# DeltaNet attention into a gated feed-forward: w_out converted in front of the second substitution, and chunk 1's first slots without feed-forward

## The chip, the cores and the metric

The kernel runs on one core of a Trainium2 chip. The metric is the device time of one execution in microseconds (us). The profile is of one further execution, taken by the hardware profiler. The engines are TensorE (PE: matmuls and, as PEld, their weight loads), VectorE (DVE), ScalarE (ACT), GpSimd (POOL) and SyncE (SP), whose instructions here are all DMAs. [...]

## The reference

There are 4 batches (b), 8 heads (h), 768 steps and a head size of 48. The attention keeps a 48x48 state for each of the 32 batch-head pairs and updates it at every step; its output, laid out as 3072 tokens of 384, goes through a feed-forward with a quick GELU. The weights arrive as 64-bit floats.

```python
k_n = k / (norm(k) + 1e-06)
for t in range(S):
    y[t] = q[t] @ state
    v_old = k_n[t] @ state
    state = state + beta[t] * outer(k_n[t], v[t] - v_old)
x = y.transpose(0, 2, 1, 3).reshape(B * S, H * D)
h = x @ w_in                       # 3072x384 @ 384x2048
out = (h / (1 + exp(-1.702 * h))) @ w_out   # 2048x384
```

## The kernel before

The 768 steps are cut into 6 chunks of 128. A *unit* is one chunk of one batch (8 heads together); units 0 to 3 are chunk 0, units 4 to 7 chunk 1, and so on up to 23. The recurrence within a chunk is a triangular system. Its matrix has four diagonal blocks of 32; these are inverted on DVE, and the rest is done by forward substitution on PE.

**Keys.** For each unit the keys are normalised in place (`normalize`, lines 301 to 315, mostly on POOL, or `normalize_mixed`, 317 to 330, on ACT and DVE), turned on PE (`turn`: tile psT, then kT), and multiplied with themselves (`gram`: psG, then G). `prepare` (402 to 434) does the last two, and sends G's diagonal blocks through DRAM (Nd) into the tile NT, one partition for each block and row group. Key tiles KN rotate through 7 buffers; a key tile is loaded by `load` (84 to 90).

**Inversion, called the second substitution for chunk 1.** `invert` (441 to 537) is a chain of DVE operations on NT and YB: multiply NT by beta, 15 rounds for the 16-wide diagonal halves, 4 + 4 rounds (`dots`) for the quarter between them, then the result YS. For chunk 0 the result is turned on DVE (YT) and scaled into XB; later chunks send YS through DRAM (Yd) into XB, the factor that the first matmul of a hop (psU) needs. `invert(0)` and `invert(1)` treat four units at once, later calls two.

**Hops.** `together` (796 to 810) is one hop: psU = XB times V for a block (`solve`, copied by ACT into U), and psR = G times U for the blocks below (`below`), which DVE subtracts from V (`rest`). Each hop needs the copy and the subtraction of the one before.

**Slots.** `woven(n, share)` (840 to 881), called slot n below, runs three hops, each serving up to three units at different blocks, and between them the work for later units: psQ of unit n+1 (line 858), `prepare` of unit n+5, rounds of `invert` (STEPS, line 837) when n is 5 or more, the outputs of unit n-1 (psY), and psT of the queries of unit n+2. `follow(n)` (812 to 827) issues loads and, for even n from 6, queues the feed-forward of a finished pair of units.

**Feed-forward.** `hidden` (700 to 722) computes the 2048 hidden values of a pair of units in 16 items of three matmuls (ph, then gT by ACT's GELU); `written` (724 to 739) and `both_written` (741 to 759) compute the outputs in 16 items of two or four matmuls (po, copied by ACT to o, stored by SP). `spend(cost)` (831 to 835) lets the queued items into a slot up to a cost of 1.3 for each item.

**Conversion.** The weights' 64-bit words are turned into float32 by `conversion` (205 to 228): one AND on DVE, one Relu on ACT, and four more DVE operations for each piece. w_in has 9 pieces, w_out 14 (`pieces`, 230 to 251); `fill` (294 to 296) emits the next operations in order. Raw slices of w_out land in places that earlier pieces leave, so most are fetched when an earlier one is done (`fetches`, 283 to 291): slice 3 after the last of w_in, 8 to 15 after slices of w_out.

**Order of the work around the change.** Nearly all of it is pinned to the order in which the code emits it. First come norms and keys of chunk 0, `invert(0)` with a block of filler matmuls (`warm`, which multiply constants and whose result nobody reads; NY = 60 of them at line 501), 8 hops for units 0 and 1, 8 hops for units 2 and 3 with hidden of the first pair between them, and `keys` (962 to 982), which works through the keys of units 4 to 8 by a table of begins. Then (lines 1033 to 1051) the rest of w_in is converted, `invert(1)` is emitted between items of hidden, and slots 3, 4, 5 ... follow, of which slots 3 to 6 carry the po items of chunk 0's two pairs, and `both_written` draws the conversion of w_out along with it. `feed` emits one item of feed-forward.

```python
    while not ("in", 3, 1) in done:
        fill(2)
        feed()
        ahead_of(preparing, 1)
```

Of the kernel before, what the change touches and what calls it, by code (L numbers as in the profile page):

```python
# [18 lines left out]
def kernel(  # L19
# [26 lines left out]
    NP = H // 2  # L46
# [8 lines left out]
    GB = 8  # L55

    XR = DP - D
    NW, NA, NY, NU = 14, 3, 60, 11
    NQ = DFF // 4
    NPC = DFF // 8  # L60
    NS = C * C + C
# [379 lines left out]
    def invert(c, b0=0, nb=B):  # L441

        np = nb * NB * H
        part = slice(b0 * NB * H, b0 * NB * H + np)
        N, Y = NT[part], YB[part]
        bc = bI[part, c].broadcast_to([np, BS, BS])
        tt, red = vec.tensor_tensor, vec.tensor_reduce
        if c > 0:
            tt(N, N, bc, op=ALU.mult)
            yield 0.0  # L450
        HS = BS // 2

        def dots(o, a, b, ny, nx, nk, negate):

            P = wk.tile([128, ny, nx, nk], F32, tag="P", name="P")[part]
            tt(P, a, b, op=ALU.mult)
            red(o, P, axis=AX.X, op=ALU.add, negate=negate)

        def halves(t):

            return [t[:, s * HS : (s + 1) * HS, s * HS : (s + 1) * HS] for s in range(2)]


        Yf = Y.rearrange("p j i -> p (j i)")
        Nf = N.rearrange("p i k -> p (i k)")
        step = HS * BS + HS

        def diag(t, off, dims):
            return bass.AP(t.tensor, t.offset + off, [t.ap[0], [step, 2]] + dims)

        for i in range(1, HS):
            P = wk.tile([128, 2, i, i], F32, tag="P", name="P")[part]
            tt(
                P, diag(Nf, i * BS, [[0, i], [1, i]]), diag(Yf, 0, [[BS, i], [1, i]]),
                op=ALU.mult,
            )
            red(diag(Yf, i, [[BS, i]]), P, axis=AX.X, op=ALU.add, negate=True)
            yield 0.0


        X1 = N[:, 0:HS, HS:]
        if c == 1:
            vec.tensor_copy(X1, halves(Y)[1].rearrange("p l i -> p i l"))
        else:
            act.activation(X1, halves(Y)[1].rearrange("p l i -> p i l"), ACT.Copy)
        A = N[:, 0:HS, 0:HS]
        N10, Y0 = N[:, HS:, 0:HS], halves(Y)[0]
        Q = 4
        for j in range(0, HS, Q):
            n = HS - j  # L490
            dots(
                A[:, j : j + Q, :],
                N10[:, :, j:].rearrange("p (o l) k -> p o l k", o=1).broadcast_to([np, Q, HS, n]),
                Y0[:, j : j + Q, j:].rearrange("p j (o k) -> p j o k", o=1).broadcast_to([np, Q, HS, n]),
                Q, HS, n, False,
            )
            yield 0.0
        for i in range(0, HS, Q):
            n = i + Q
            if c == 0 and i == HS - 2 * Q:  # L500
                warm(NY, vec.memset)
            dots(
                Y[:, 0:HS, HS + i : HS + i + Q],
                A[:, :, 0:n].rearrange("p j (o l) -> p j o l", o=1).broadcast_to([np, HS, Q, n]),
                X1[:, i : i + Q, 0:n].rearrange("p (o i) l -> p o i l", o=1).broadcast_to([np, HS, Q, n]),
                HS, Q, n, True,
            )
            yield 0.0
        if c == 0:
            T = wk.tile([128, BS, BS], F32, tag="P", name="YT")  # L510
            vec.transpose(T.rearrange("p d i -> p i d"), Y.rearrange("p j i -> p i j"))
            for b in range(B):
                XB = wk.tile([128, H, BS], F32, tag="XB", name="XB", bufs=4)
                tt(
                    XB, T[:, b * H : (b + 1) * H],
                    zs[:, 5, b].broadcast_to([128, H, BS]), op=ALU.mult,
                )
                inverse[b] = XB
                yield 0.0
            return  # L520
        YS = wk.tile([128, BS, BS], F32, tag="P", name="YS")[part]
        tt(YS, Y, bc, op=ALU.mult)
        dma = sync if c < 3 else nc.sync.dma_start
        groups = [range(b0, b0 + nb)]
        back = {}
        for bs in groups:
            for b in bs:
                back[b] = dram.tile([H * C, BS], F32, tag="Yd", name="Yd", bufs=4)
                dma(
                    out=back[b].rearrange("(p j) i -> p j i", j=BS),  # L530
                    in_=YS[(b - b0) * NB * H : (b - b0 + 1) * NB * H],
                )
            for b in bs:
                XB = wk.tile([128, H, BS], F32, tag="XB", name="XB", bufs=4)
                dma(out=XB, in_=back[b].rearrange("(h t) i -> t h i", h=H))
                inverse[c * B + b] = XB
        yield 0.0
# [162 lines left out]
    def hidden(xT, gT, t, cost, gated=False):  # L700

        n = t.stop - t.start
        for f0 in range(0, FC, 2):
            if f0 // FQ == len(gT):
                gT.append(wk.tile([128, FQ, NTH], F32, tag="gT", name="gT", bufs=GB))
            if gated:
                while not ready_in(f0):
                    fill(1)
            ph = ps_moe.tile([128, 2, n], F32, tag="moe", name="ph")
            for u in range(2):  # L710
                f = f0 + u
                for j in range(KC):
                    pe.matmul(
                        ph[:, u], lhsT=w_in[:, j, f * 128 : (f + 1) * 128], rhs=xT[:, j, t],
                        start=(j == 0), stop=(j == KC - 1),
                    )
                if u == 0:
                    yield cost
            act.activation(
                gT[f0 // FQ][:, f0 % FQ : f0 % FQ + 2, t], ph, ACT.Gelu_apprx_sigmoid  # L720
            )
            yield cost
# [48 lines left out]
    def run(work):  # L771
        for _ in work:
            pass
# [38 lines left out]
    def follow(n):  # L812

        dma = sync if n <= B else nc.sync.dma_start
        if n + B < len(units):
            load(n + B, ((QP, q),), dma)
        m = n - 1 + len(KN)
        if m < len(units):
            load(m, ((KN, k),), nc.gpsimd.dma_start)
        if n - 1 + B < len(units):  # L820
            load_values(n - 1 + B, dma)
        if n % HB == 0 and n > B:
            h = (n - 1) // HB
            gT = []
            queue.append(hidden(xTs[h], gT, slice(0, NTH), 1.3))
            queue.append(written(*units[h * HB], gT))
            xTs.pop(h)

    debt = [0.0]

    def spend(cost):

        debt[0] = debt[0] + cost if queue else 0.0
        for done in take(debt[0]):
            debt[0] -= done
# [71 lines left out]
    for b in range(B):  # L907
        load_values(b, sync)
    fetch_in(1, other_queue)
    D_ = spare("blocks").rearrange("p (b h k) -> p b h k", b=B, k=BS)  # L910
    fetch_in(2, other_queue)
    for n in range(B, len(KN)):
        load(n, ((KN, k),), sync)
# [13 lines left out]
    norms_first()  # L927
    for e in range(2):
        vec.tensor_tensor(
            D_[:, :, e::2], psD[e], zs[:, 5, :, e::2].broadcast_to([128, B, NP, BS]), op=ALU.mult  # L930
        )
    vec.transpose(
        NT.rearrange("p i k -> p k i"), D_.rearrange("p b h k -> p k (b h)")
    )
    for b in range(B):
        gram(b)
# [25 lines left out]
    def keys():  # L962

        def unit(n):
            yield from normalize_mixed(n)
            yield from prepare(n)

        begun[2 * B] = prepare(2 * B)

        def first(n):  # L970
            yield from normalize_mixed(n)
            next(begun[n])

        work = [unit(n) for n in range(B, 2 * B)] + [first(2 * B)]
        for t in range(26):
            for u, begin in enumerate((0, 3, 6, 14, 17)):
                s = t - begin
                if s >= 0 and s % 2 == 0:
                    next(work[u], None)
            yield  # L980
        for w in work:
            run(w)
# [43 lines left out]
    for s in pair[2:]:  # L1026
        put_out(s)
        feed()
        fill(2)
    ffn.append(hidden(xTs[1], gTs[1], slice(0, NTH), 1.3, True))  # L1030
    xTs.pop(0), xTs.pop(1)
    load(B + 2, ((QP, q),), sync)
    while not ("in", 3, 1) in done:
        fill(2)
        feed()
        ahead_of(preparing, 1)
    run(preparing)
    first = new_step(B)
    run(first.scored)
    inverting = invert(1)  # L1040
    for i in range(25):
        ahead_of(inverting, 1)
        feed()
    run(inverting)
    fill(5)
    while ffn:
        feed()
    queue = [both_written(0, gTs[0]), written(*units[HB], gTs[1])]
    for n in range(B - 1, len(units) + 1):
        woven(n, 20.8 if n > 6 else 10.4)  # L1050
    run(take(1e9))
# [31 lines left out]
```

## Time and profile before

| what | value |
|---|---|
| median of 3 runs | 792.73 us (790.88 to 793.82) |
| profiled execution: its own time | 792.6 us |
| profiled execution: span, first to last instruction | 790.9 us |
| mean granted TensorE clock | 0.965 of full |
| PE busy, 0 to 51 us (norms, first inversion) | 39.7 of 51.05 us, clock 0.67 |
| PE busy, 51 to 103 us (hops of chunk 0) | 49.5 of 51.75 us |
| PE busy, 103 to 121 us (hidden, rest of w_in) | 17.6 of 18.6 us |
| DVE busy, 103 to 121 us | 13.0 of 18.6 us |
| filler matmuls | 199 |

The table of stages gives, for each stretch, the time that each engine was busy and in brackets its instructions, then the clock that was granted to TensorE, the share of the DMA engines and the rate of transfer. A line of the timeline gives start, duration, engine, source line, operation, tiles written and read, their shapes and the count, and in square brackets how long the engine had been idle before it and what released it. Line 102 is a helper through which most instructions pass, so groups are told apart by tile. The trace counts a float32 matmul as two records.

### The profile page before, as it was taken

What the parts mean: (1) busy time and instruction counts of PE and PEld (TensorE: products, weight loads), DVE (VectorE), ACT (ScalarE), POOL (GpSimd) and SP (SyncE); (2) the same over time, 40 slices, a digit from 0 to 9 for tenths busy, and PEclk for the clock granted to TensorE, in tenths of its full rate; (3) what the DMA queues carried; (4) which work ended last, traced back from release to release, by engine and by line L of the source; (5) the groups of instructions that cost most, each with busy time, mean ns of one, the idle gap of its engine ahead of it and who ended that gap; (6) DMA issues with size and microseconds to landing.
All of it is one profiled execution on the core that took longest, in us unless ns stands there. A gap on an engine that the chain in (4) does not pass through costs nothing.

```text
span 790.9 us, 18899 instructions
## 1 busy us (share of the span) xinstructions
PE 754.1 (95%) x8199; PEld 564.5 (71%) x8199; DVE 456.5 (58%) x934; ACT 243.0 (31%) x537; POOL 127.1 (16%) x132
## 2 busy tenths in 40 slices
PE   7788999598899999999999999999999999999997
PEld 6677888355568768768678678678678678677684
DVE  6778778996895666766666766756756531100000
ACT  4555552244233323223223223223223123121110
POOL 6301410001121212212212211221210000000000
PEclk8589999799999999999999999999999999999999
DMA  9941940453323231231222232241230020000000
GB/s 164 176 58 39 256 96 8 111 162 72 75 64 70 55 86 42 58 90 35 64 74 52 56 95 43 46 103 42 46 76 12 21 43 2 12 15 1 25 1 20
DMA packets 130657, 50.72 MB, mean 64 GB/s; under 512 B 105408, under 2 KB 126016, under 8 KB 130576
## 3 DMA queue, kind: packets, MB, share of 16 engines
q1 hardware_dynamic: 128112, 41.08, 24.1%
q0 software_dynamic: 2464, 8.46, 4.4%
q8 instruction: 64, 1.05, 0.6%
q14 instruction: 17, 0.14, 0.1%
HBM read 32.08 MB, written 16.25 MB: 61 GB/s over the span
## 4 chain that ended last, share of the span: by engine, by line
PE 81%; DVE 12%; DMA 3%; ACT 2%; issue 2%; SPq 1%; POOL 0%; DVEq 0%; POOLq 0%; ACTq 0%
PE po L102 28%; PE ph L102 26%; PE psY L102 5%; PE psU L102 5%; PE psQ L102 4%; PE psG L102 4%; PE ps_warm L102 3%; PE psT L102 3%; DVE P L102 3%; DVE YB L102 2%; DVE w_out L102 2%; PE psR L102 2%; DVE tmp L102 2%; DMA Nd<-G 1%; DVE NT L102 1%
## 5 line engine op out<-in xcount | busy, mean ns | idle before, releaser
L102 PE MATMUL po<-w_out,gT 128*128 128x384 f32 x768 | 269.5, 500 | 11.7 <-ACT w_out L102 8.9
L102 PE MATMUL ph<-xT,w_in 128*128 128x256 f32 x1152 | 261.5, 383 | 0.3
L102 PEld LDWEIGHTS ph<-xT,w_in 128*128 128x128 f32 x1152 | 214.7, 190 | 32.7 <-issue 1.5
L102 PEld LDWEIGHTS po<-w_out,gT 128*128 128x128 f32 x768 | 143.1, 193 | 103.9 <-ACT w_out L102 9.3
L102 DVE TENSOR_TENSOR V<-V,psR 64x384 f32<-64x384 f32 (+1 forms) x96 | 53.4, 556 | 198.0 <-PE psR L102 192.7
L102 ACT ACTIVATE gT<-ph 128x512 f32<-128x512 f32 x96 | 56.5, 596 | 140.1 <-PE ph L102 140.0
L102 DVE TENSOR_TENSOR P<-NT,YB 64x8 f32<-64x8 f32 (+31 forms) x190 | 89.2, 469 | 5.3
L102 ACT COPY US<-psU 32x384 f32<-32x384 f32 x92 | 43.2, 469 | 146.1 <-PE psR L102 128.6
L102 DVE TENSOR_REDUCE YB<-P 64x4 f32<-64x8 f32 (+31 forms) x190 | 80.9, 426 | 6.5
L102 PEld LDWEIGHTS psU<-V,XB 32*32 32x32 f32 x1536 | 57.9, 106 | 35.4 <-issue 29.0
L102 PE MATMUL psU<-V,XB 32*32 32x48 f32 x1536 | 68.6, 204 | 1.5 <-DVE YB L102 1.2
L605 POOL TENSOR_SCALAR_AFFINE_SELECT M<-M 128x1024 f32<-128x1024 f32 x20 | 24.9, 1247 | 265.9 <-DVE M L102 169.4
L102 PE MATMUL psR<-US,G 32*32 32x48 f32 x2208 | 60.4, 204 | 0.0
L102 PEld LDWEIGHTS psR<-US,G 32*32 32x32 f32 x2208 | 51.1, 106 | 1.1 <-ACT G L102 0.5
L102 PE MATMUL psQ<-QS,kT 48*128 48x176 f32 (+1 forms) x384 | 37.6, 341 | 3.7 <-ACT QS L102 3.7
L102 DVE TENSOR_TENSOR P<-NT 64x256 f32<-64x256 f32 (+7 forms) x40 | 34.0, 851 | 4.8 <-ACT NT L102 4.6
L102 PEld LDWEIGHTS psQ<-QS,kT 48*128 48x128 f32 x384 | 31.1, 209 | 6.8 <-ACT QS L102 5.6
L102 PE MATMUL ps_warm<-ident 128*128 128x256 bf16 x199 | 29.9, 309 | 5.4 <-DVE ps_warm L102 4.0
L102 PE MATMUL psG<-kT 48*128 48x128 f32 x384 | 32.3, 306 | 2.6 <-ACT kT L102 1.3
L102 DVE TENSOR_REDUCE NT<-P 64x64 f32<-64x1024 f32 (+7 forms) x40 | 32.6, 815 | 1.4
L87 POOL DMA_DIRECT2D KN<-in_k_dram x15 | 14.3, 951 | 111.5 <-PE psY L102 102.6
L102 PEld LDWEIGHTS psG<-kT 48*128 48x128 f32 x384 | 27.3, 205 | 6.0 <-ACT G L102 2.1
(98 smaller groups left out, 604.2 us busy)
## 6 DMA issues: line engine op xcount, KB each, us to landing
Nd<-G SPq DMA_DIRECT2D x16, 512.0 KB, 3.5
QP<-in_q_dram SPq DMA_DIRECT2D x24, 192.0 KB, 3.8
V<-in_v_dram SPq DMA_DIRECT2D x24, 192.0 KB, 3.3
out_dram<-o SPq DMA_DIRECT2D x24, 192.0 KB, 1.9
KN<-in_k_dram POOLq DMA_DIRECT2D x15, 192.0 KB, 3.7
NT<-Nd SPq DMA_DIRECT2D x20, 128.0 KB, 2.5
Yd<-YS SPq DMA_DIRECT2D x20, 128.0 KB, 2.4
XB<-Yd SPq DMA_DIRECT2D x20, 128.0 KB, 3.3
```

The costliest lines, as they stand in the source:

```text
L87: dma(out=dst[n % len(dst)][:, :, 0:D], in_=src[b, :, c * C : (c + 1) * C, :].rearrange("h p d -> p h d"),)
L102: return lambda *a, **kw: tc.keep_in_program_order(op(*a, **kw))
L605: (pool if self.n < B else nc.gpsimd).affine_select(out=self.M, in_=self.M, compare_op=ALU.is_gt, fill=0.0, base=0, pattern=[[0, H], [1, 1 ...
```

## The change

Six things change.

1. **Fillers at the start.** 48 filler matmuls in place of 60, released one round of the loop earlier (the third of the last four rounds from the end instead of the second).
2. **Layouts of two DVE transposes.** The tile YT is now written densely and read with a stride by the four operations after it; the tile "blocks" is written with a stride by the two operations before its transpose and read densely by it.
3. **Keys of units 7 and 8** begin 4 steps earlier in `keys`, and it has 22 steps instead of 26.
4. **Keys of units 9 and 10** are loaded by SP ahead of the slots, instead of by POOL in `follow`, and normalised ahead of `invert(1)` by `more_keys`; unit 9's are also turned there. Slots 4 and 5 then find `prepare` begun.
5. **All of w_out is converted ahead of `invert(1)`**, with both hiddens and both po passes of chunk 0 between the operations; scores of unit 4 (psT, psQ) come at the start of that loop.
6. **Slots 3 to 6 have no feed-forward.** `spend` emits fillers (3.8 for each unit of cost, 37 in a slot) until `follow(6)` queues the first pair of chunk 1.

```diff
-    NW, NA, NY, NU = 14, 3, 60, 11
+    NW, NA, NY, NU = 14, 3, 48, 11
...
-            if c == 0 and i == HS - 2 * Q:
+            if c == 0 and i == HS - 3 * Q:
                 warm(NY, vec.memset)
...
-            vec.transpose(T.rearrange("p d i -> p i d"), Y.rearrange("p j i -> p i j"))
+            vec.transpose(T, Y.rearrange("p j i -> p i j"))
+            T = T.rearrange("p i d -> p d i")
...
         m = n - 1 + len(KN)
-        if m < len(units):
+        if 2 * B + HB < m < len(units):
             load(m, ((KN, k),), nc.gpsimd.dma_start)
...
             gT = []
+            ffn_begun.append(h)
             queue.append(hidden(xTs[h], gT, slice(0, NTH), 1.3))
...
-    debt = [0.0]
+    debt, ffn_begun = [0.0], []
 
     def spend(cost):
 
+        if not queue and not ffn_begun:
+            warm(int(cost * 3.8))
         debt[0] = debt[0] + cost if queue else 0.0
...
-    D_ = spare("blocks").rearrange("p (b h k) -> p b h k", b=B, k=BS)
+    D_ = spare("blocks").rearrange("p (k d) -> p k d", k=BS)
...
-            D_[:, :, e::2], psD[e], zs[:, 5, :, e::2].broadcast_to([128, B, NP, BS]), op=ALU.mult
+            D_.rearrange("p k (b h) -> p b h k", b=B)[:, :, e::2], psD[e], zs[:, 5, :, e::2].broadcast_to([128, B, NP, BS]), op=ALU.mult
...
-        NT.rearrange("p i k -> p k i"), D_.rearrange("p b h k -> p k (b h)")
+        NT.rearrange("p i k -> p k i"), D_
...
-        for t in range(26):
-            for u, begin in enumerate((0, 3, 6, 14, 17)):
+        for t in range(22):
+            for u, begin in enumerate((0, 3, 6, 10, 13)):
...
     ffn.append(hidden(xTs[1], gTs[1], slice(0, NTH), 1.3, True))
+    ffn.append(both_written(0, gTs[0]))
+    ffn.append(written(*units[HB], gTs[1]))
     xTs.pop(0), xTs.pop(1)
     load(B + 2, ((QP, q),), sync)
-    while not ("in", 3, 1) in done:
+    for n in range(2 * B + 1, 2 * B + 1 + HB):
+        load(n, ((KN, k),), sync)
+    first = new_step(B)
+    next(first.scored)
+
+    def more_keys():
+
+        n = 2 * B + 1
+        yield from normalize_mixed(n)
+        yield from normalize_mixed(n + 1)
+        begun[n], begun[n + 1] = prepare(n), prepare(n + 1)
+        next(begun[n])
+        yield
+
+    later = more_keys()
+    t = 0
+    while len(done) < len(list(pieces())):
         fill(2)
         feed()
-        ahead_of(preparing, 1)
+        if t == 0:
+            run(first.scored)
+        if t < 18:
+            ahead_of(preparing, 1)
+        elif t % 2 == 0:
+            ahead_of(later, 1)
+        t += 1
     run(preparing)
-    first = new_step(B)
-    run(first.scored)
+    run(later)
     inverting = invert(1)
-    for i in range(25):
+    for i in range(36):
         ahead_of(inverting, 1)
         feed()
     run(inverting)
-    fill(5)
     while ffn:
         feed()
-    queue = [both_written(0, gTs[0]), written(*units[HB], gTs[1])]
     for n in range(B - 1, len(units) + 1):
         woven(n, 20.8 if n > 6 else 10.4)
```

The order of the built program shows what follows from it on PE: ph of chunk 0, 12 matmuls of po, psT of unit 9, 52 of po, 13 fillers, then slot 3's psU; and on SP the four stores of chunk 0's outputs stand ahead of Yd and XB of units 4 to 7.

## The prediction

> **What bounds the kernel now.** I read the granted clock first (0.965), then the engine table, then the busy time stage by stage, then the order of time on each engine from 100 to 250 us. All times are from the span's start.
>
> ```profile
> PE 754.1 (95%) x8199; PEld 564.5 (71%) x8199; DVE 456.5 (58%) x934; ACT 243.0 (31%) x537; POOL 127.1 (16%) x132
> core 0: us, PE busy (x) PEld busy (x) DVE busy (x) ACT busy (x) POOL busy (x), PEclk, DMA share, GB/s
> 121.40:148.10 26.70, 20.04 (x93) 17.29 (x91) 25.26 (x50) 4.78 (x8) 0.00 (x0) 0.96 0.00 1
> 148.10:170.60 22.50, 18.72 (x120) 10.68 (x120) 21.77 (x43) 7.56 (x13) 0.00 (x0) 0.82 0.65 168
> 170.60:193.30 22.70, 19.07 (x201) 11.48 (x201) 17.04 (x40) 9.86 (x22) 3.00 (x2) 0.92 0.38 100
> 193.30:216.30 23.00, 20.62 (x283) 13.66 (x284) 18.29 (x47) 6.43 (x17) 4.61 (x3) 0.93 0.41 95
> 246.60:738.00 491.40, 491.05 (x5309) 367.07 (x5306) 261.67 (x535) 135.90 (x297) 76.39 (x60) 1.00 0.20 48
> ```
>
> From 246.6 us TensorE (PE) is never idle, and its order from slot 7 on is the same in both programs. So whatever the change does shows as a shift of one event: slot 7's middle hop, psU of unit 8, at 245.80. ("Slot n" is one call of woven(n); "the inversion" is invert(), the substitution.) Before that event, PE loses time only where VectorE (DVE) is full:
>
> ```profile
> 121.43 1.23 DVE L102 TENSOR_TENSOR NT<-NT,bI 128x1024 f32<-128x1024 f32 x1 [3.05 <-issue]
> 150.37 7.11 PE L102 MATMUL po<-w_out,gT 128*128 128x384 f32 x12 [8.93 <-ACT w_out L102]
> 157.40 0.86 PE L102 MATMUL psU<-V,XB 32*32 32x48 f32 x16
> 186.56 0.56 DVE L102 SCALAR_TENSOR_TENSOR w_out<-tmp,w_out 128x384 f32<-128x384 f32 x1
> 187.42 1.16 PE L102 MATMUL psG<-kT 48*128 48x128 f32 x16
> 189.72 0.37 SPq L102 DMA_DIRECT2D Nd<-G  x1
> 194.20 0.34 SPq L102 DMA_DIRECT2D NT<-Nd  x1
> 196.70 2.06 DVE L102 TENSOR_TENSOR NT<-NT,bI 64x1024 f32<-64x1024 f32 x1 [0.22 <-DMA NT<-Nd]
> 234.20 1.70 DVE L102 TENSOR_TENSOR YS<-YB,bI 64x1024 f32<-64x1024 f32 x1
> 245.80 0.20 PE L102 MATMUL psU<-V,XB 32*32 32x48 f32 x1 [1.20 <-DVE YB L102]
> ```
>
> Read them as DVE's sequence: chunk 1's inversion (121.4 to 148.1), conversion of w_out (148.0 to 187.1) with slots 3 and 4 beside it, then the inversion of units 8 and 9 (196.7 to 235.9), which could start only after unit 9's keys: psG at 187.4, two DMAs, 8.15 us. The 8.9 us hole in PE before 150.4 is what the change can fill.
>
> [...] the 60 fillers from 41.8 took 9.33 us, where 11 at full clock take 1.31, so some 5.3 us of them ran at half rate; and 12 records of po after the 8.9 us hole took 7.1 us. [...] the transposes, strided on both sides, take 1.94 to 1.96 us for 1024 elements where other operations take 1.22, while a strided COPY of 256 took 0.39, no more than a dense one. Only which side costs is not shown.
>
> **The change part by part.** Every time below is in the new program unless said.
>
> *Start (fillers, transposes).* The memset that releases the fillers moves up one round of its loop, 41.60 - 40.27 = 1.3 us. Twelve fillers fewer at 1.31/11 = 0.12 us are 1.4 us. First psU: 51.05 - 2.7 = 48.4; the first of the four XB operations ends at 48.00 + 0.36 = 48.4 too, so 2.6 us are gained and no more. The transposes: each side of each layout made dense may give 0.7 us (1.95 - 1.22), and writing "blocks" with a stride may cost as much for its 1024 elements; together -1.4 to +0.7, I take 0. Gain 2.6 (1.6 to 3.5).
>
> *Keys of units 7 and 8 sooner.* psG (1.1) and psT (0.45) move from behind the second put_out to before it. PE is busy throughout 80 to 110, so the sum stays; the inversion's NT is in place long before DVE wants it, and its idle 115.1 to 121.4 (6.3, less 0.8 of V<-V,psQ moved ahead of it) goes. What is late next is the conversion itself.
>
> *Feed-forward of chunk 0 in one run.* After the put_outs PE has 26 items of hidden at 1.29 (6 records in 1.49 less 0.2 of overlap), psT and psQ: 102.8 + 1.5 + 33.5 + 1.9 - 2.6 = 137.1. Then 32 items of po at 1.29 (64 records in 20.66) and psT of unit 9: 178.9. The 8.9 us hole and its 3 us of cold clock are gone.
>
> *w_out before the inversion.* Last w_in operation 115.1 + 0.8 + 1.0 (psG and psT ahead of it in the hops) - 2.6 = 114.3. Fourteen pieces: four at 2.34, doubles 3.79 and 3.59, eight at 2.22, less the first operation already done: 34.2. Keys of 9 and 10: 2 x 1.4. About 1 us of waits, as each Relu stands on ACT behind a gT copy that PE frees every 2.58 us, and slice 3 is fetched only at 114 with 6.3 to land on POOL's queue. End 152.3. The inversion, 26.65: 179.0. The fetches of slices 8 to 15 and keys 9, 10 go ahead on SP's queue as far ahead of use as now, cost 0.
>
> *A new wait.* On SP's queue the four output stores now stand ahead of Yd. The last waits for po (178.9) and its copy (0.48), so Yd is issued at 180.1 instead of 179.0. Yd to XB took 2.0 at 148.10, XB lands in 3.3: first psU of unit 4 at 185.6 to 186, taken 186 (183.5 to 188). PE's 13 fillers end at 180.5; it has then been idle over 5 us and is cold.
>
> *Slots 3 and 4 alone.* Slot 3 on PE: psU 0.43, psG 1.1, psR 0.85, psT 0.45, 24 fillers 2.9: 5.7, plus 2.4 for the cold start, 8.1 (5.7 to 9). Slot 4 to the end of psG of unit 9: psU 0.43, psQ 1.4, 13 fillers 1.55, psU and psR 0.85, 6 fillers 0.7, psG 1.1: 6.0. Then the 8.15 us through Nd and NT, with no cover left (7.1 the next time they run). NT at 186 + 8.1 + 6.0 + 8.1 = 208.2, 11.5 later than 196.7. DVE has nothing from 179 but the V updates of these slots.
>
> *Slots 5, 6, to slot 7's hop.* From NT to YS DVE took 39.2; less idle 2.6, unit 10's norm 0.9 (made earlier) and 0.8 (2.06 instead of 1.22 for NT): 34.9. New waits 1.6: V of slot 5 stands behind eight rounds of inversion, so PE stops some 4.7 us ahead of slot 5's third hop, turns cold, and psY and psG come late to DVE. YS to Yd to psU: 7.1 from Yd's issue at 238.72. Together 43.6 (42 to 46): 251.8. PE's own work, with 6 items of ph, would be there by about 250, so it doesn't bind.
>
> **Sum.** 251.8 - 245.8 = +6.0. Against its own time of 792.6 (span 790.9 and 1.7 around it) that is 798.6; the median of the runs, 792.73, is as good as the same, so 798.5. Bounds: 183.5 + 5.7 + 6 + 7.1 + 42 = 244.3, -1.5; 188 + 9 + 6 + 8.2 + 46 = 257.2, +11.4.
>
> **Rivals.**
> B, no change: the clock stays up in the slots, the DMAs run at their medians (Nd 3.5, NT 2.5) and YS leaves at once. 184.5 + 6 + 6 + 7.3 + 43 = 246.8: +1, 793.7. For it: NT's chain took 7.1 at 234.7. Against: the idle ahead of slot 3 is longer than the 2.4 us after which psT and po slowed at 204.3.
> C, faster: without feed-forward the hops run as in chunk 0, 2.11 us each with 11 fillers; unit 9's psG is then reached after four hops, 8.4 instead of 14.1. With XB at 183.5 and NT's chain at 7.1, NT is at 199 and the hop at 241.2: -4.6, 788.0. It decides from NT before 202 (245.8 - 43.6). Against: psQ, psG and 37 fillers a slot stand on PE between those hops.
> D, worse: the clock stays low through slots 3 to 6, as it did from 20 to 40 us (0.50). Their 24 us of PE work cost up to half as much again where DVE doesn't cover it, slots 3 and 4 some 6 more: +12, 804.6.
> That the change doesn't do what it says is out: in the new order all po of chunk 0 precede slot 3.
>
> **Numbers.** Forecast 0.55, B 0.20, C 0.16, D 0.09. A measurement here tells 0.5% (4 us) from no change. Slower: 0.09 and all of the forecast but its lower edge, and a little of B, 0.62; same 0.21; faster 0.17. The forecast's own range is 794 to 803; the range for 8 in 10 goes down to 789 and up to 804.
>
> **What would show it.** Right: PE without a hole from 105 to 179; conversion ended near 152, the inversion's YS near 179; PE idle about 5 us ahead of slot 3 with a lower clock; DVE idle most of 180 to 208, with NT (64x1024) near 208; PE idle before slot 5's third hop; slot 7's psU of unit 8 near 252, and all behind it shifted alike. Wrong: NT before 202, or the conversion of w_out stalled by its fetches or by ACT beyond 156, or the start gaining more than 3.5.

## The result and the profile after

The changed kernel takes 816.76 us (median of 4 runs, 813.55 to 819.74) against 791.83 of the kernel before, timed beside it: a ratio of 1.031, with a 95% interval of 1.027 to 1.036. The forecast was 798.5, with 789 to 804 for 8 in 10. Slower was the right side, but the loss is 25 us and not 6. The profiled execution has a span of 815.3 us and its own time is 817.3.

The first part of the page of the changed kernel, busy time by engine:

```profile
PE 779.5 (96%) x8335; PEld 588.0 (72%) x8335; DVE 454.9 (56%) x934; ACT 243.1 (30%) x537; POOL 123.5 (15%) x130
```

PE's busy time has grown by 25.4 us over the kernel before, though the fillers added (335 instead of 199) are worth 16 us at full clock (0.12 each). The rest goes with a lower clock in some stages (0.84 and 0.70 in the last two of the table below, 0.88 and 0.96 in the kernel before). That PE is busy for 96% of the time says nothing here; stages do. The table of stages of the changed kernel, cut at first psU, at 103, at the end of the second substitution (YS), at NT of units 8 and 9 and at the end of their substitution:

```profile
core 0: us, PE busy (x) PEld busy (x) DVE busy (x) ACT busy (x) POOL busy (x), PEclk, DMA share, GB/s
49.03:103.00 53.97, 48.24 (x934) 38.97 (x934) 39.06 (x69) 25.58 (x48) 12.26 (x12) 0.91 0.49 115
103.00:189.86 86.86, 84.89 (x389) 60.77 (x390) 74.81 (x150) 25.73 (x50) 6.15 (x4) 1.00 0.23 63
189.86:221.62 31.76, 27.36 (x456) 22.04 (x455) 5.00 (x15) 9.84 (x24) 2.18 (x2) 0.84 0.54 112
221.62:261.16 39.54, 30.71 (x474) 24.86 (x471) 32.50 (x67) 10.45 (x26) 6.31 (x5) 0.70 0.25 56
```

The same stages of the kernel before:

```profile
51.05:103.00 51.95, 49.67 (x995) 41.10 (x995) 38.56 (x69) 26.32 (x52) 13.23 (x13) 0.97 0.50 119
103.00:148.08 45.08, 37.45 (x196) 32.15 (x194) 38.01 (x71) 14.07 (x27) 2.54 (x3) 0.98 0.17 38
148.08:196.70 48.62, 41.19 (x372) 24.90 (x373) 40.69 (x88) 19.12 (x39) 3.10 (x3) 0.88 0.53 135
196.70:235.90 39.20, 36.59 (x550) 24.57 (x550) 34.77 (x70) 12.46 (x30) 10.03 (x7) 0.96 0.29 66
```

Take the length of each stretch less DVE's busy time. DVE has the same work up to the substitution of units 8 and 9 in both (152.0 and 151.4 us), and its idle time is 13.4 + 7.1 + 7.9 + 4.4 = 32.8 before and 14.9 + 12.0 + 26.8 + 7.0 = 60.7 after. That is 27.9 us more idle DVE; less 2.0 us of an earlier start and 0.6 of less work it is the 25.3 by which YS of units 8 and 9 ends later (261.16 against 235.90). Behind it, everything is shifted alike: from that YS to the end it is 555.0 us before and 554.1 after, and between 552.4 and 555.0 in all runs below. So one number, the end of this YS, tells each kernel's time, and DVE's idle time tells in which stage it was lost. This is bookkeeping; what caused the idle time is for the experiments to show.

Where the idle time starts shows in the timeline of the changed kernel on SP, ACT and PE from 73 us:

```profile
73.27 5.64 SPq L102 DMA_DIRECT2D w_out<-in_moe_w_in_dram  x12
76.94 0.47 ACT L102 COPY US<-psU 32x384 f32<-32x384 f32 x1 [0.47 <-PE psR L102]
79.06 2.24 SPq L102 DMA_DIRECT2D KN<-in_k_dram  x2
84.92 0.52 ACT L102 ACTIVATE ksq<-KN 128x384 f32<-128x384 f32 x1 [7.51 <-DMA KN<-in_k_dram]
85.46 1.08 ACT L102 ACTIVATE G<-psG 128x512 f32<-128x512 f32 x2
86.11 0.85 PE L102 MATMUL psT<-ident,KN 128*128 128x128 f32 x4 [2.77 <-ACT G L102]
88.51 2.93 PE L102 MATMUL ph<-xT,w_in 128*128 128x256 f32 x6
```

The same load and its first square in the kernel before:

```profile
82.35 1.01 SPq L102 DMA_DIRECT2D KN<-in_k_dram  x2
90.70 0.53 ACT L102 ACTIVATE ksq<-KN 128x384 f32<-128x384 f32 x1
```

Key tiles of units 7 and 8 are issued on SP behind twelve transfers of raw w_in, at 79.06 (in the kernel before, behind the same twelve, at 82.35). The squares (ksq) of these tiles now come two hops sooner on ACT, at 77.4 in its queue, and the tile has not landed. ACT stands for 7.5 us, and behind it in its queue stand the copy of G and the copy U that the hop needs. psG is done at 80.6 and its copy G starts at 85.46, at the end of the square, where the copy before it, at 74.53, had started 0.03 us after its psG; U follows at 86.57. So a copy that was ready waited 4.9 us for a square that was not. PE waits, and soon after it resumes it runs at half rate, with a granted clock of 0.5 from 86.4 to 93.3: six ph take 2.93 us where the six at 81.35 took 1.56 at full clock.

The timeline of the changed kernel on the prediction's later steps:

```profile
124.19 23.55 PE L102 MATMUL ph<-xT,w_in 128*128 128x256 f32 x108 [1.16 <-DVE w_in L102]
163.25 1.22 DVE L102 TENSOR_TENSOR NT<-NT,bI 128x1024 f32<-128x1024 f32 x1
188.64 1.22 DVE L102 TENSOR_TENSOR YS<-YB,bI 128x1024 f32<-128x1024 f32 x1
190.98 1.77 SPq L102 DMA_DIRECT2D Yd<-YS  x4
195.78 1.49 PE L102 MATMUL psU<-V,XB 32*32 32x48 f32 x16 [4.40 <-DMA XB<-Yd]
203.55 1.14 DVE L102 TENSOR_TENSOR V<-V,psR 32x384 f32<-32x384 f32 x2 [13.68 <-PE psR L102]
211.75 1.16 PE L102 MATMUL psG<-kT 48*128 48x128 f32 x16
221.62 1.22 DVE L102 TENSOR_TENSOR NT<-NT,bI 64x1024 f32<-64x1024 f32 x1 [2.65 <-DMA NT<-Nd]
227.36 0.25 PE L102 MATMUL psU<-V,XB 32*32 32x48 f32 x1 [4.64 <-DVE V L102]
262.54 8.04 PE L102 MATMUL ph<-xT,w_in 128*128 128x256 f32 x36
262.95 0.33 SPq L102 DMA_DIRECT2D NT<-Nd  x1
263.37 2.12 SPq L102 DMA_DIRECT2D Yd<-YS  x2
270.51 0.23 PE L102 MATMUL psU<-V,XB 32*32 32x48 f32 x2
```

The order is as forecast: no hole in PE from 124 to the end of po, conversion and substitution one behind the other, an idle PE ahead of slot 3, DVE idle (13.7 us at once) behind the substitution, the stop before slot 5's third hop. The times are not: the conversion ends at 163.3 (forecast 152.3), first psU of unit 4 is at 195.8 (186), NT of units 8 and 9 at 221.6 (208.2), slot 7's psU of unit 8 at 270.5 (251.8).

### The profile page after: what moved, and what is told of

Read it like the earlier page. It is cut to its first block, busy times and chain, and to the rows that moved or that the text cites. A ratio compares the mean times of both kernels' runs of the same rounds, so it can differ in the third digit from the quotient of the medians.

```text
span 815.3 us, 19170 instructions
## 1 busy us (share of the span) xinstructions
PE 779.5 (96%) x8335; PEld 588.0 (72%) x8335; DVE 454.9 (56%) x934; ACT 243.1 (30%) x537; POOL 123.5 (15%) x130
## 4 chain that ended last, share of the span: by engine, by line
PE 88%; DVE 5%; DMA 3%; ACT 2%; issue 1%; SPq 0%; DVEq 0%; ACTq 0%
PE po L102 31%; PE ph L102 29%; PE psY L102 6%; PE psU L102 5%; PE psQ L102 4%; PE psG L102 4%; PE ps_warm L102 4%; PE psT L102 3%; PE psR L102 2%; DVE P L102 1%; DMA KN<-in_k_dram 1%; DVE w_in L102 1%; DVE YB L102 1%; DVE tmp L102 1%; DMA Nd<-G 1%
## 5 line engine op out<-in xcount | busy, mean ns | idle before, releaser
L102 PE MATMUL po<-w_out,gT 128*128 128x384 f32 x768 | 259.5, 490 | 0.0
L102 PEld LDWEIGHTS psU<-V,XB 32*32 32x32 f32 x1536 | 59.7, 108 | 39.9 <-issue 33.2
L102 PE MATMUL psU<-V,XB 32*32 32x48 f32 x1536 | 70.5, 207 | 9.8 <-DVE V L102 4.9
L102 PE MATMUL psR<-US,G 32*32 32x48 f32 x2208 | 62.2, 208 | 0.0
L102 PE MATMUL ps_warm<-ident 128*128 128x256 bf16 x335 | 53.8, 317 | 4.1 <-DVE ps_warm L102 2.7
L102 PEld LDWEIGHTS <-ident 128*128 128x128 bf16 x335 | 35.6, 112 | 15.4 <-issue 4.4
L102 PE MATMUL psG<-kT 48*128 48x128 f32 x384 | 35.7, 329 | 2.6 <-ACT kT L102 1.3
L102 ACT COPY o<-po 128x384 f32<-128x384 f32 x24 | 11.5, 479 | 89.0 <-PE po L102 49.6
L102 PEld LDWEIGHTS psQ<-QS,kT 48*128 48x128 f32 x384 | 31.1, 209 | 7.8 <-ACT QS L102 6.6
L102 PEld LDWEIGHTS psG<-kT 48*128 48x128 f32 x384 | 30.5, 228 | 6.3 <-ACT G L102 2.1
## 6 DMA issues: line engine op xcount, KB each, us to landing
QP<-in_q_dram SPq DMA_DIRECT2D x24, 192.0 KB, 3.9
V<-in_v_dram SPq DMA_DIRECT2D x24, 192.0 KB, 3.4
out_dram<-o SPq DMA_DIRECT2D x24, 192.0 KB, 1.9
KN<-in_k_dram POOLq DMA_DIRECT2D x13, 192.0 KB, 3.6
```

The source lines that it names most:

```text
L102: return lambda *a, **kw: tc.keep_in_program_order(op(*a, **kw))
```

## The experiments

Every kernel was timed with the kernel before beside it, and the medians of before (790.3 to 791.8) differ a little. So the table gives the difference to the median of before that was timed with it, and in brackets the 95% interval of the ratio. "YS" is the end of the substitution of units 8 and 9 in the profiled execution, "DVE idle" the sum over the four stretches above, each kernel cut at its own events.

| run | median us | against before (95%) | YS | DVE idle |
|---|---|---|---|---|
| changed kernel | 816.76 | +24.9 (1.027 to 1.036) | 261.2 | 60.7 |
| begins as before | 804.83 | +13.8 (1.014 to 1.018) | 250.9 | 50.4 |
| keys loaded sooner | 807.96 | +16.9 (1.016 to 1.023) | 255.1 | 54.7 |
| no fillers in slots | 811.01 | +20.0 (1.022 to 1.026) | 255.9 | 54.8 |
| begins and no fillers | 801.64 | +11.3 (1.012 to 1.022) | 245.3 | 44.1 |
| that, layouts as before | 801.42 | +11.1 (1.011 to 1.019) | 247.2 | 46.9 |
| that pair, po in the slots | 809.59 | +19.2 (1.020 to 1.029) | 253.9 | 52.3 |
| before + begins alone | 794.85 | +4.5 (1.004 to 1.007) | 242.8 | 40.7 |
| before + start alone | 788.42 | -2.6 (0.994 to 0.998) | 232.6 | 31.1 |
| start, 15 operations ahead | 786.08 | -4.2 (0.993 to 0.997) | 229.0 | 27.0 |
| start, 40 operations ahead | 795.96 | +5.6 (1.005 to 1.009) | 241.8 | 39.3 |
| 15 ahead, unit 9's keys | 783.78 | -6.5 (0.990 to 0.995) | 228.2 | 25.3 |

**Begins as before** in the changed kernel:

```diff
-        for t in range(22):
-            for u, begin in enumerate((0, 3, 6, 10, 13)):
+        for t in range(26):
+            for u, begin in enumerate((0, 3, 6, 14, 17)):
```

> The changed kernel with the table of begins in the key stage as it was: units 7 and 8 at steps 14 and 17, 26 steps. Theory T1 (ACT stands in front of a key tile that has not landed, the hops of units 2 and 3 wait behind it, the clock falls, and the loss is carried to the end): no wait of ksq on KN longer than 1 us between 80 and 95 us, the hops of chunk 0 end 7 to 9 us sooner, and the time falls from 816.8 to 807 to 810. Rival R1 (it is the psG and psT of two more units among the hops that cost, not the load): the same gain here, but none in the run that only moves the load. Rival R2 (the early loss is covered later, by the chain of slots 3 to 6): hops sooner, time within 3 us of 816.8.

Measured: 804.83, below T1's 807 to 810: more comes back than it said. The timeline of this kernel:

```profile
88.06 0.53 ACT L102 ACTIVATE ksq<-KN 128x384 f32<-128x384 f32 x1
138.37 8.21 PE L102 MATMUL po<-w_out,gT 128*128 128x384 f32 x24
186.63 1.48 PE L102 MATMUL psU<-V,XB 32*32 32x48 f32 x16 [4.46 <-DMA XB<-Yd]
213.13 1.22 DVE L102 TENSOR_TENSOR NT<-NT,bI 64x1024 f32<-64x1024 f32 x1 [2.69 <-DMA NT<-Nd]
259.01 0.20 PE L102 MATMUL psU<-V,XB 32*32 32x48 f32 x1 [0.79 <-DMA XB<-Yd]
```

No wait at ksq, po begins at 138.4 (147.6 in the changed kernel), and psU of unit 4 is at 186.6. R2 falls: the 9.2 us saved early arrive whole at psU of unit 4, and 10.3 at YS.

**Keys loaded sooner**, begins left at 10 and 13:

```diff
     for s in pair[:2]:
         put_out(s)
+        load(7 + s.n, ((KN, k),), sync)
         fill(2)
-    load(7, ((KN, k),), sync)
-    load(8, ((KN, k),), sync)
```

> The changed kernel with only the loads of the keys of units 7 and 8 moved on SP's queue: each right behind its put_out, ahead of the 12 transfers of raw w_out that stand before them now. The begins stay at 10 and 13. T1: the 7.5 us wait of ksq on KN is gone, the clock of 70 to 103 us is back above 0.92, and the time falls to 807 to 810; as the keys are still sooner, perhaps 1 us better than with the begins of before. R1: time within 3 us of 816.8. R2: the wait gone, hops sooner, time within 3 us of 816.8.

Measured: 807.96, within T1's 807 to 810, and R1 as the only cause falls. But the clock of 70 to 103 us stayed at 0.84, against the expectation, and at psU of unit 4 (192.0) this kernel regains only 3.8 of the 9.2 us; 2.3 more come in the slots. The timeline of this kernel:

```profile
78.98 2.08 PE L102 MATMUL psG<-kT 48*128 48x128 f32 x16
82.42 2.90 PE L102 MATMUL ph<-xT,w_in 128*128 128x256 f32 x6
```

With the wait gone, the last update of the state of units 2 and 3 is at 105.6, where it is at 100.2 with the old begins. The trace shows two reasons: psG at 79 and the six ph after it ran at half rate (2.08 and 2.90 us, against 1.16 and 1.56), and psG and psT of the sooner units stand among the last hops, with a wait for ACT's copy of G between them. The half rate began at 74.9 (granted clock 0.75 from 70 to 80 us and 0.74 from 80 to 90), ahead of the moved work on PE, and the profiled execution took 809.96 where the four go from 804.85 to 809.96, so some of it may be chance. By the medians the moved load alone gives back 8.0 of the 11.1 us that the old begins give back, and is the larger part of the loss; with four runs of each the split is rough.

**The begins alone**, in the kernel before (the two lines of the first diff, reversed):

> The kernel before with the table of begins alone as in the changed kernel (10 and 13, 22 steps). T1: ACT waits 6 to 8 us for a key tile near 80 us, the hops of units 2 and 3 end 7 us later, the start of the second substitution 5 us later, and the time rises by 4 to 9 us, to 794.5 to 800. Rival, the prediction's own step (the sum of PE's work stays, and NT is only sooner): within 1.5 us of before, or up to 4 us faster, as the second substitution finds its NT sooner.

Measured: 794.85, +4.5, at the lower edge of T1's range; the step that the prediction took at nothing costs by itself. The timeline of this kernel (the profiled execution took 799.24; the twenty go from 791.87 to 799.24):

```profile
85.82 0.52 ACT L102 ACTIVATE ksq<-KN 128x384 f32<-128x384 f32 x1 [8.63 <-DMA KN<-in_k_dram]
87.02 1.12 PE L102 MATMUL psT<-ident,KN 128*128 128x128 f32 x4 [5.18 <-ACT G L102]
```

The same wait. It costs less here than the 11.1 us between the first two rows of the table. A reason that the trace offers, and that was not tried by itself: in the kernel before DVE stands idle for 3.1 us ahead of the second substitution, which is gone here, so part of the delay goes into that slack; in the changed kernel the conversion stands in front of that substitution, and there is no slack.

**No fillers in slots 3 to 6** of the changed kernel:

```diff
     def spend(cost):
 
-        if not queue and not ffn_begun:
-            warm(int(cost * 3.8))
         debt[0] = debt[0] + cost if queue else 0.0
```

> The changed kernel without the fillers in slots 3 to 6. If the fillers only stand in the path of those hops (37 in a slot, 0.12 us each at full clock and 0.24 at half), the event psU of unit 8 comes 3 to 6 us sooner and the time is 811 to 814. If they keep the clock up, as they are meant to, the slots turn colder and the time is 817 to 823. If DVE and the transfers set the pace there, within 2 us of 816.8.

Measured: 811.01, the first of the three. The table of stages of this kernel, from the end of the second substitution to NT of units 8 and 9, and from there to YS:

```profile
189.33:215.87 26.54, 20.86 (x340) 18.17 (x343) 5.00 (x15) 9.07 (x22) 1.09 (x1) 0.54 0.62 134
215.87:255.86 39.99, 26.02 (x473) 22.01 (x464) 33.97 (x67) 11.90 (x29) 8.43 (x6) 0.62 0.24 53
```

Read it beside the changed kernel's two lines: the clock falls from 0.84 to 0.54, as the fillers' purpose would have it, and still the first stretch is 5.2 us shorter. The fillers keep the clock up in that stretch and cost more than the clock brings. They stand on PE between hops whose chain sets the pace.

**Both undone.** The edits are the first and the last diff together.

> The changed kernel with two parts undone together: the begins in the key stage as before, and no fillers in slots 3 to 6. If the two losses lie one behind the other on the path, the savings measured singly (12.0 and 5.8 us) add up: 816.8 - 17.8 = 799, which is where the prediction stood. If they share a cause (the clock), less than the sum is saved: 801 to 805. If fillers are needed once the hops are sooner, 805 or more.

By the profile the two savings add up: YS ends 15.9 us sooner than in the changed kernel, where the single ones give 10.3 and 5.3. The median saves 13.6 against 11.1 + 4.9 = 16.0, in the window for a shared cause, but the runs scatter from 800.0 to 806.6, too widely to tell the two apart.

**Layouts as before**, on top:

```diff
-            vec.transpose(T, Y.rearrange("p j i -> p i j"))
-            T = T.rearrange("p i d -> p d i")
+            vec.transpose(T.rearrange("p d i -> p i d"), Y.rearrange("p j i -> p i j"))
...
-        NT.rearrange("p i k -> p k i"), D_
+        NT.rearrange("p i k -> p k i"), D_.rearrange("p b h k -> p k (b h)")
```

> As the run with both parts undone, and the two layouts (YT and blocks) as before too. The trace says that each dense side saved nothing on the transpose and that each strided side cost 0.6 us: 1.2 us to be had, so 0.8 to 1.5 us below the run with both undone. The prediction took 0, with bounds of -1.4 to +0.7 for the new layouts: then it is the same or up to 1.4 slower.

Measured: 801.42, no difference that these runs can tell: 1.2 us is within their scatter. The first psU is 0.9 us sooner (47.97 against 48.92), but that is no proof, as it lies anywhere from 48.2 to 49.0 in the other profiles with the new layouts, and from 47.9 to 48.7 in those with the new start and the old layouts. What the layouts do to DVE shows in the timeline of the changed kernel's start:

```profile
13.01 1.90 DVE L102 TENSOR_TENSOR blocks<-psD,zs 128x512 f32<-128x512 f32 x2
14.94 1.93 DVE L102 STREAM_TRANSPOSE NT<-blocks 128x1024 f32<-128x1024 f32 x1
46.36 1.95 DVE L102 STREAM_TRANSPOSE YT<-YB 128x1024 f32<-128x1024 f32 x1
48.34 2.07 DVE L102 TENSOR_TENSOR XB<-YT,zs 128x256 f32<-128x256 f32 x4
```

Before, the four lines were 1.29, 1.94, 1.96 and 1.43. A dense side saved the transposes nothing, and the strided side that moved to the neighbour cost 0.6 us each time, 1.2 us on DVE in all.

**The start alone**, in the kernel before:

```diff
-    NW, NA, NY, NU = 14, 3, 60, 11
+    NW, NA, NY, NU = 14, 3, 48, 11
...
-            if c == 0 and i == HS - 2 * Q:
+            if c == 0 and i == HS - 3 * Q:
```

> The kernel before with the start alone: 48 fillers instead of 60, released at the third of the last four rounds; layouts as before. By the prediction's step first psU comes at 48.4 instead of 51.05 and, as PE is the bound behind it, the time falls by 2 to 2.6 us, to 789.3 to 790. Rival: the inversion's chain on DVE (XB of the first unit at 51.05 less the waits) sets it, and less than 1 us is gained; or the clock is not yet full after 48, and nothing is.

Measured: 788.42, -2.6 us, with an interval of 1.6 to 4.6 us sooner: as forecast. One profile would not have shown it. The first psU is at 48.17 here and at 51.05 in the kernel before, but at 49.05 in the kernel with the begins alone, whose start is the old one: its 60 fillers took 8.0 us, and those of the kernel before 9.3.

**The po of chunk 0 in the slots**, on the version with begins and fillers undone:

```diff
-    ffn.append(both_written(0, gTs[0]))
-    ffn.append(written(*units[HB], gTs[1]))
...
     while ffn:
         feed()
+    queue = [both_written(0, gTs[0]), written(*units[HB], gTs[1])]
     for n in range(B - 1, len(units) + 1):
```

> As the run with both parts undone (801.6), but the po of chunk 0 stays in the slots, as in the kernel before, while w_out is still converted ahead of the second substitution. It asks which half of the change costs: the order of conversion and substitution on DVE, or the empty slots. If the order costs (the chain from XB of unit 4 to NT of units 8 and 9 no longer has the conversion beside it), the time stays at 800 to 806: PE's po ride in the slots, some 6 us of them stand ahead of psG of unit 9, the warmer clock gives about half of that back. If the empty slots cost, the time falls to 795 or less.

Measured: 809.59, above both expectations. The empty slots are not what costs here: with po in them it is 8 us worse. The timeline of this kernel:

```profile
184.35 1.48 PE L102 MATMUL psU<-V,XB 32*32 32x48 f32 x16 [42.53 <-DMA XB<-Yd]
217.59 1.21 DVE L102 TENSOR_TENSOR NT<-NT,bI 64x1024 f32<-64x1024 f32 x1
```

PE stands empty for 42.5 us ahead of slot 3 and that alone costs nothing, as psU is at 184.4 (187.0 with po ahead). From psU of unit 4 to NT of units 8 and 9 it is then 33.2 us, against 20.8 with empty slots and 26.5 with fillers. In these three kernels whatever stands on PE between those hops, useful or not, lengthens the one chain that DVE waits for.

**How much of the conversion ahead.** In the kernel with the start alone, operations of w_out's conversion put ahead of the second substitution, 15 or 40 of them:

```diff
     first = new_step(B)
+    fill(5)
     run(first.scored)
+    fill(10)
     inverting = invert(1)
```

The kernel with 40 has 35 in place of 10.

> The kernel before with the start alone, and 15 operations of w_out's conversion put into the idle time of DVE ahead of the second substitution (5 ahead of the scores of unit 4, 10 behind them), the rest of the conversion where it was. If DVE's idle time there is free (7 us between 110 and 118.6 in the run with the start alone), the conversion ends 5 to 6 us sooner and the time is 783 to 785. If the wait for unit 9's keys behind the conversion takes it back, 787 to 788.5. If the Relus on ACT or the filling delay NT, above 788.5.

> As the run that fills DVE's idle time, with 40 operations of w_out ahead of the second substitution instead of 15: some 11 us of conversion more than the idle time holds, so units 4 to 7 get XB about 11 us later, and the rest of the conversion (about 15 us) still lies beside slots 3 and 4. If conversion ahead is only dear once too little of it is left to lie beside the chain from XB to NT (some 25 us), the time is 787 to 791, between the run with 15 (786.1) and the changed order (801). If any conversion beyond the idle time costs its own length, 795 to 798. If it is free, 785 to 787.

Measured: 786.08 with 15 and 795.96 with 40. The first is between its two cases (DVE's idle time from 103 us to the end of the second substitution went from 8.7 to 4.3), and its 1.6 us beyond the start alone lie within the intervals of the two. The second refutes the first of its cases and is in the range of the second, that conversion beyond the idle time costs its own length: 25 operations more put NT of the second substitution 13.8 us later (135.00 against 121.17) and YS of units 8 and 9 12.8. The timeline of the kernel with 40:

```profile
166.24 1.48 PE L102 MATMUL psU<-V,XB 32*32 32x48 f32 x16 [6.56 <-DMA XB<-Yd]
176.63 1.14 DVE L102 TENSOR_TENSOR V<-V,psR 32x384 f32<-32x384 f32 x2 [12.83 <-PE psR L102]
```

From psU of unit 4 to the first subtraction in V it is 10.4 us here, and 10.6 in the kernel with the start alone (153.61 to 164.20), where conversion filled them. Now DVE stands idle for 12.8 us, although a third of the conversion was still to do: its operations come in DVE's list behind that subtraction. So it was not enough here that work was left; it had to stand ahead of the wait in the same list. The changed order puts all of the conversion ahead, and shows the same idle stretch (13.7 us).

**Unit 9's keys sooner, feed-forward left in the slots**, on the kernel with 15 ahead (the load by SP behind the put_outs, in place of POOL's, is left out of the diff):

```diff
     for i in range(25):
         ahead_of(inverting, 1)
         feed()
+        if i in (8, 12, 16):
+            next(norm9)
+        if i == 20:
+            next(begun[n9])
...
         run(P)
+        if n == B - 1:
+            next(begun[2 * B + 1])
```

> As the run that fills the idle time, and unit 9's keys sooner in a way that leaves the feed-forward in the slots: loaded by SP behind the put_outs, normalised and turned among the operations of the second substitution, multiplied in slot 3. The substitution of units 8 and 9 then finds NT there when the conversion ends, and 7 us of idle DVE (185.6 to 193 in the run with the start alone) go. If DVE is the bound up to slot 7, 776 to 780. If PE takes its place (it has some 12 us of holes between 137 and 200 to give), 780 to 784. If the transfers of NT ahead of raw w_out on SP's queue stall the conversion, 785 or more.

Measured: 783.78, the middle case, and faster than both kernels: 0.992 of the kernel before, 0.990 to 0.995. How much of it is due to the keys stays open, as the interval overlaps with that of the kernel with 15 ahead. The table of stages of this kernel:

```profile
103.00:149.38 46.38, 39.48 (x184) 32.78 (x182) 42.59 (x83) 14.94 (x29) 3.58 (x3) 0.96 0.24 60
149.38:188.91 39.53, 33.84 (x355) 21.58 (x356) 32.95 (x70) 16.43 (x34) 1.27 (x1) 0.88 0.63 149
```

DVE is idle 3.8 and 6.6 us in these two stretches, where it was 7.1 and 7.9 before and 12.0 and 26.8 in the changed kernel.

## Why the prediction was wrong

What held: the bound (DVE's sequence up to the substitution of units 8 and 9, then a plain shift), the start (2.6 forecast, 2.6 measured alone), the length of the conversion with its keys (38.0 forecast; some 39 between the last w_in operation and NT), the 1.1 us that the stores put in front of Yd (189.86 to 190.98), the idle and cold PE ahead of slot 3 (4.40 us idle, the granted clock 0.5 from 195.7 to 205.9), and the 4.7 us stop in slot 5 (4.64). The layouts were taken at 0 and made no difference that the times can tell, though not as argued: the transposes gained nothing at all, and DVE's lines took 1.2 us more, beyond the +0.7 that the prediction allowed.

The step that failed is "*Keys of units 7 and 8 sooner*": "PE is busy throughout 80 to 110, so the sum stays". It priced the moved step by PE's work alone. The step also has a square on ACT, which reads a tile that SP issues behind twelve transfers, and ACT's queue also carries the hops' copies. So ACT stood for 7.5 us, and the hops with it. The prediction looked at where the moved instructions go on PE and DVE and not at when their data land. With that step undone, psU of unit 4 is at 186.6, where the forecast had 186, and po starts at 138.4, where it had 137.1. It is 11.1 of the 24.9 us by the medians.

The second term is "*Slots 3 and 4 alone*", 8.1 + 6.0 + 8.1 = 22.2 from psU of unit 4 to NT; 25.8 were measured, and 26.5 with the begins as before. Mechanism and sign were right, the size was not: to the end of psG of unit 9 it is 17.1 us (195.78 to 212.91) where the sum had 14.1, and Nd and NT take 8.7 for 8.1. The sum had 2.4 us for a cold start, the author's estimate, and 43 fillers at full clock (5.2 us); in the trace all of slot 3 runs at half rate, fillers included (psU 1.49 us; 0.86 comes back only at 206.5). Without fillers the stretch is 20.8 us. Rival D, a low clock through slots 3 to 6, described this part, but its +12 was for all of them.

The third is "*Slots 5, 6, to slot 7's hop*", 43.6 forecast and 48.9 measured (221.62 to 270.51); it is 45.9 with the begins as before (213.13 to 259.01). Its sum has a hole: it goes from NT to the end of YS and then on from Yd's issue, and leaves out what lies between, 2.8 us in the kernel before (235.90 to 238.72) and 2.2 in the changed one (261.16 to 263.37). On SP, Yd stands behind the transfer of NT of a later unit, issued at 262.95. From Yd's issue to psU it is the 7.1 us of the sum, but PE's own work does bind at the end: it is on 36 records of ph up to 270.5 and waits for no XB, where with the begins as before it waits for 0.8 us. The other 3.0 us are DVE's, 39.5 from NT to YS for 36.5. That the same code took 1.8 us less there with the begins as before goes with the granted clock, 0.82 against 0.70; why the clock differs between them stays open.

By slot 7's psU of unit 8 the miss of 18.7 us (270.5 against 251.8) is thus 11.5 for the begins and 7.2 for the rest: 0.6 to psU of unit 4, 4.3 from there to NT, 2.3 behind it. With begins and fillers undone that psU is at 253.7. That its NT is then at 207.8, so near the 208.2 of the forecast, is luck: the sum had 43 fillers that this kernel lacks, and a warmer clock than its 0.57. The medians are 11.3 us above before, against the +6 forecast (8.1 between the two profiled executions, 800.67 and 792.6). What remains is at its core the chain from psU to NT without the conversion beside it, as the runs with 40 operations and with po in the slots indicate; the keys of units 9 and 10 were not put back by themselves. Rival C (faster) asked for NT before 202; with all of the conversion ahead none came below 207.8. By its own figures its hop would have been at 199 + 43.6 = 242.6, not 241.2.

## What to carry to other kernels

When a step is moved up, follow each of its instructions on its own engine to the data it reads: the new place in the queue against the landing of the tile, on the issuing queue's own order. A wait that was harmless on an idle engine here (PE's 42.5 us ahead of slot 3 with po in the slots) was not so on one that also carries the copies of a dependent chain (ACT's 7.5 us for a key tile). And before work is moved out of the shadow of a chain of waits, ask what else will stand in that shadow: DVE's idle time up to the bound's end, summed by stages, gave the time of each profiled execution here within 2.5 us.

## What the runs showed of the hardware

From the end of the second substitution to NT of units 8 and 9 a higher granted clock went with a longer stage: 0.84 and 31.8 us with fillers (changed kernel), 0.54 and 26.5 us without.

In the profiles of the kernel before and of the changed kernel the granted clock changes only at points that lie a multiple of 3.41 us apart (11 and 15 changes). Take the steps of 3.41 us at full clock from 40 us on: there are 9 in which PE was busy for less than 1.9 us, and half clock followed each; of the other 412, one was followed by half clock (2.2 us busy, up to 76.2 in the changed kernel). In the changed kernel PE was busy for 0.65 us of the step up to 86.4, with the wait for ACT in it, and the clock was half from there to 93.3. In three of the 9 PE was idle throughout; in the others its waits added up to 1.6 to 2.8 us. This is a reading of two profiles; no run was made for it.

A transpose of 128x1024 took 1.92 to 1.97 us, whether one side was dense or both were strided, while operations that write or read with the stride in its stead took 1.90 for 1.29 us (two of 512) and 2.07 for 1.43 (four of 256). Each of these transposes has at least one strided side; one with both sides dense was not run.
